# G = pp @ w for two f tiles in one step, the attention's small products next to it, the output product in thirds of K

## The chip, the core and the metric

One core of a Trainium2 chip. TensorE (PE) multiplies into PSUM; VectorE (DVE), ScalarE (ACT) and GpSimd (POOL) do the rest of the arithmetic, and SyncE (SP) issues the DMAs. The metric is the device time of one execution in microseconds (us). Before the change it is 772.41 us, the median of three runs (771.77 to 772.71).

## The reference

Eight batches of eight heads, sequence 576, head size 64. Per head, 32 packed queries `p` attend to `k`, `v`, and the queries `q` attend to what they gave; the result is the input of a gated feed-forward layer. All is float32.

```python
p_packed = sm_attn(p, k, v)            # (8, 8, 32, 64)
out = sm_attn(q, p_packed, p_packed)   # (8, 8, 576, 64)
x = out.transpose(0, 2, 1, 3).reshape(4608, 512)
return ((x @ w_a) * (x @ w_b)) @ w_out # w_a, w_b: 512 x 1536; w_out: 1536 x 512
```

## The kernel before

The second attention's weights, times `p_packed`, times `w_a`, are regrouped: G = pp @ w is built first (32 packed rows of each of eight heads, so 256 rows in two halves e of 128), and then x @ w_a and x @ w_b are a2 @ G, where a2 are the softmax weights of the second attention. The 1536 columns are cut into twelve f tiles of 128. Products of full precision are made of float32r parts, hi and lo: three matmuls for each product (hi hi, hi lo, lo hi).

Batches 0 and 1 run in an earlier stage of another form. The change concerns the loop over batches 2 to 7, which is written in *periods*, one for each f tile, 72 in all (`period`, L803). A period n holds

- `make_g` (L764): G of tile n + 2, eight small matmuls (L772) of 64 rows by 32 columns with 256 columns moving (128 for w_a, 128 for w_b), four heads r and two halves e, into the PSUM pair `s`;
- `sum_g` (L778): ACT, DVE and POOL form the sums `gs` that a product scheme with seven instead of eight block products needs; `split_g` (L788) cuts them into G_hi and G_lo, a third of a period later;
- seven block products (`product`, L754, matmuls at L759) of tiles n and n + 1 into the PSUM pairs `X` and `V`, each three matmuls with 288 columns;
- the steps that end a tile: d (ACT L821, DVE L824), c2 (ACT L832, DVE L847), the two halves of h = a * b, which are hf[1] on DVE (L837) and hf[0] on POOL (L848), and `split_h` (L793) of the tile before into h_hi (ACT L800) and h_lo (POOL);
- three *fills*: matmuls of the output product h @ w_out (`mm2_steps`, L718, matmuls at L722 with 512 columns), which run behind by half a batch. They accumulate six f tiles (half of K) of one 128-row tile in a bank of the PSUM pool `x` (two banks). The first half is copied by ACT to `part` (L728), the second is added to it by DVE (L732) and stored.

The next batch's attention is spread over the twelve periods by the strings in `STEPS` (L861), at three places in a period: behind the first, second and third fill. In them S is the first attention's score product (L255), r its following steps (the last of them the product with v, L299, all in the PSUM pair `s`), s the second attention's steps, the first of which is a product (L314), k and q transpositions on DVE, u the splitting of a2 into parts for the next batch (DVE a_lo and tx_lo, through `lo_part`, L92), t sums on POOL, L loads. The order on each engine is that in which this code is written (a manual schedule). G's weights are kept in DRAM (`w_kept`) by batch 1 and loaded for each f tile (`load_kept`, L698), 512 KB, into one of two buffers.

Of the kernel before, what the change touches and what calls it, by code (L numbers as in the profile page):

```python
# [8 lines left out]
F32 = mybir.dt.float32  # L9
# [10 lines left out]
def tile_packed_attn_gated_ffn(  # L20
# [568 lines left out]
    def keep_weights():  # L589

        c, u = divmod(kept[0], 2)
        nc.sync.dma_start(
            out=w_kept[kept[0]].rearrange("p (x f) -> p x f", f=P),
            in_=w_ab[:, c].rearrange("p r (a u f) -> p (r a) u f", a=2, u=2)[:, :, u, :])
        kept[0] += 1
# [38 lines left out]
    def tiles_of(b):  # L634
        return [64 + P * i for i in range(4)] if b % 2 == 0 else [P * i for i in range(5)]

    for b in range(NB):
# [33 lines left out]
        for i, c0 in enumerate(tiles):  # L671
# [7 lines left out]
            mm2_out(b, banks[i], c0, i)  # L679
    while kept[0] < NFT:  # L680
        keep_weights()
# [10 lines left out]
    part = lp.tile([P, NT, DO], F32, name="part")  # L692
    a_t = {(e, u): tuple(t[:, e, HS * u:HS * u + HS] for t in (a2_hi, a2_lo)) for e in range(E) for u in range(2)}
# [12 lines left out]
    load_kept(1)  # L706

# [9 lines left out]

    def mm2_steps(o, c0, fts, cols=slice(0, DO)):  # L718

        for ft in fts:  # L720
            for n, (ht, wt) in enumerate(((h_hi[ft], wo_hi[ft]), (h_hi[ft], wo_lo[ft]), (h_lo[ft], wo_hi[ft]))):
                nc.tensor.matmul(  # L722
                    out=o[:, cols], lhsT=ht[:, c0:c0 + P], rhs=wt[:, cols],
                    start=(ft == fts[0] and n == 0), stop=(ft == fts[-1] and n == 2))
                yield

    def keep_part(o, i):
        nc.scalar.copy(out=part[:, i], in_=o)  # L728

    def put_out(b, o, i, c0):  # L730
        ob = lp.tile([P, DO], F32, name="ob", bufs=2)
        nc.vector.tensor_tensor(out=ob, in0=o, in1=part[:, i], op=ALU.add)  # L732
        store(b, ob, c0)

    def mm2_half(b, half, tiles=None):

        for i, c0 in tiles or list(enumerate(tiles_of(b))):
            o = bank()
            yield from mm2_steps(o, c0, range(HF * half, HF * half + HF))
            if half == 0:  # L740
                pend.append(lambda o=o, i=i: keep_part(o, i))
            else:
                pend.append(lambda o=o, i=i, c0=c0: put_out(b, o, i, c0))

    filler = [iter(())]

    def fill(k):

        for _ in range(k):
            next(filler[0], None)  # L750
# [3 lines left out]
    def product(n, k, bank, first):  # L754

        j, (hi, lo) = PRODUCTS[k]
        gh, gl = G_hi[:, n % 3, j], G_lo[:, n % 3, j]
        for i, (g, t) in enumerate(((gh, hi), (gh, lo), (gl, hi))):
            nc.tensor.matmul(  # L759
                out=bank[:, n % 2, 0:HS], lhsT=g, rhs=t, start=(first and i == 0), stop=(i == 2), skip_group_check=True)  # L760
# [3 lines left out]
    def make_g(n):  # L764

        b = NB + n // NFT
        w = wr_of.pop(n)
        x = bank_pair(True)
        for r in range(R):
            for e in range(E):  # L770
                rows = slice(64 * e, 64 * e + 64)
                nc.tensor.matmul(  # L772
                    out=x[J * r:J * r + J, e, 0:2 * P], lhsT=ppT[rows, 2 * (b % 2), r, :], rhs=w[rows, r, :],
                    start=True, stop=True)
        load_kept(n + 2)
        return x

    def sum_g(n, x):  # L778

        nc.scalar.copy(out=gs[:, 0:2].rearrange("p a f -> p (a f)"), in_=x[:, 1, 0:2 * P])  # L780
        nc.scalar.copy(out=G_hi[:, n % 3, 0], in_=x[:, 0, 0:P])  # L781
        nc.vector.tensor_tensor(out=gs[:, 4], in0=x[:, 0, P:2 * P], in1=gs[:, 1], op=ALU.add)  # L782
        nc.vector.tensor_tensor(out=gs[:, 5], in0=gs[:, 4], in1=x[:, 0, 0:P], op=ALU.subtract)  # L783
        lo_part(G_lo[:, n % 3, 0], x[:, 0, 0:P], G_hi[:, n % 3, 0])
        nc.gpsimd.tensor_tensor(  # L785
            out=gs[:, 2:4], in0=gs[:, 0:2], in1=gs[:, 5:6].broadcast_to([P, 2, P]), op=ALU.subtract)

    def split_g(n):  # L788

        nc.scalar.copy(out=G_hi[:, n % 3, 1:7], in_=gs)  # L790
        lo_part(G_lo[:, n % 3, 1:7], gs, G_hi[:, n % 3, 1:7], nc.gpsimd)

# [10 lines left out]
    def period(n, fills, steps):  # L803
# [15 lines left out]
        if here or there:  # L819
            d = d_of[n] = lp.tile([P, 2, HS], F32, name="d", bufs=2)  # L820
            nc.scalar.copy(out=d[:, both], in_=X[:, both, 0:HS])  # L821
        fill(fills[0])
# [3 lines left out]
        emit_steps(b + 1, steps[0])  # L826
        if here:
# [17 lines left out]
        if here:  # L845
            c2 = c2_of.pop(n)
            nc.vector.tensor_tensor(out=c2, in0=V[:, k0, 0:HS], in1=c2, op=ALU.add)  # L847
            nc.gpsimd.tensor_tensor(out=hf[:, 0], in0=d_of.pop(n - 1)[:, k0], in1=c2, op=ALU.mult)  # L848
# [12 lines left out]
    STEPS = {0: ("S0 r0", "", "Lq1"), 1: ("S1 r1", "r0", ""), 2: ("r0", "r1", ""), 3: ("r0", "", "q0 Lv1"),  # L861
             4: ("r1", "", "q1 Lk2"), 5: ("r1", "P0", "Lv2 Lk3"), 6: ("s0 s0", "T2", "Lp4 s0"), 7: ("s1 s1", "s0", "s1"),
             8: ("s0", "s1", "s0"), 9: ("s1", "", "s1 t"), 10: ("", "u0", "u1 k2"), 11: ("", "u2", "u3 k3 Lq2")}
    banks_of["x"], banks_of["v"] = bank_pair(), bank_pair()
    for n in (-2, -1):
        period(n, (12, 12, 12) if n == -2 else (10, 8, 9), ("", "", ""))
    for n in range(LAST):
        b, ft = NB + n // NFT, n % NFT
        if ft % HF == 0:
            fill(99)  # L870
            flush()
            half_b = b if ft else b - 1
            filler[0] = mm2_half(half_b, 0 if ft else 1)
        period(n, (6, 4, 5) if half_b % 2 else (5, 3, 4), STEPS[ft])
    split_h(LAST - 1)
    fill(99)
    flush()
    last, tiles = B - 1, list(enumerate(tiles_of(B - 1)))
    filler[0] = mm2_half(last, 1, tiles[:-1])
    for _ in range(10):  # L880
        fill(9)
        flush()
    i, c0 = tiles[-1]
    ob = lp.tile([P, DO], F32, name="ob", bufs=2)
    for j in range(2):
        o = bank()
        cols = slice(j * DO // 2, (j + 1) * DO // 2)
        drain(mm2_steps(o, c0, range(HF, NFT), cols))
        nc.vector.tensor_tensor(out=ob[:, cols], in0=o[:, cols], in1=part[:, i, cols], op=ALU.add)
        store(last, ob, c0, cols)  # L890

# [29 lines left out]
```

## Time and profile before

| | |
|---|---|
| median of the runs | 772.41 us |
| the profiled execution | 773.32 us |
| its span, first to last instruction | 771.2 us |
| mean granted TensorE clock | 0.991 |
| PE busy with matmuls | 735.8 us |
| POOL / DVE / ACT busy | 471.8 / 420.6 / 362.8 us |
| moved by DMA | 102.47 MB, mean 133 GB/s |

Busy time is time in which an instruction of the engine is shown. Matmuls are pipelined: one starts before the one ahead is shown to end, so what a matmul costs is read from start to start. The loop of the periods runs from about 194 us to 740 us of the span; behind it stands the rest of the last batch's output product.

### The profile page before, as it was taken

Reading aid. Unit: us, or ns where it says so; the run is one execution under the profiler, and the core shown is the slowest. Engines: PE = TensorE matmul, PEld = TensorE weight load, DVE = VectorE, ACT = ScalarE, POOL = GpSimd, SP = SyncE. Lnnn points to the kernel's source line nnn. Section 1 sums busy time; section 2 is a strip of 40 time slices with the busy share of each in tenths; the row PEclk is TensorE's granted clock in tenths of the full one; section 3 lists DMA queues with packets and bytes.
Section 4 is the critical chain, followed back from the end, with each engine's and each line's share of the span. In section 5 each row is a group of like instructions: output and inputs, shape, how many; then the busy total and the mean of one; then the engine's idle time right before and its main releaser. Section 6 shows DMA issues by size and latency. Waiting matters only on the chain.

```text
span 771.2 us, 15740 instructions
## 1 busy us (share of the span) xinstructions
PE 735.8 (95%) x6140; PEld 573.5 (74%) x6140; DVE 420.6 (55%) x832; ACT 362.8 (47%) x760; POOL 471.8 (61%) x394
## 2 busy tenths in 40 slices
PE   6899999997999998999999998999999999899998
PEld 4488878975778766777777776677777777688887
DVE  2888564466245556555664556655664555544321
ACT  3778634533343454544544354453454335544430
POOL 0586652335165795667866688566875668777640
PEclk9999999998999999999999999999999999999999
DMA  8999937694335515373253732448144322123002
GB/s 247 376 239 290 247 68 155 161 245 127 86 108 147 162 60 116 110 183 109 83 119 111 184 120 74 104 136 189 68 107 107 118 107 83 55 96 124 28 1 69
DMA packets 193866, 102.47 MB, mean 133 GB/s; under 512 B 141953, under 2 KB 172417, under 8 KB 193793
## 3 DMA queue, kind: packets, MB, share of 16 engines
q1 hardware_dynamic: 193792, 101.47, 47.9%
q8 instruction: 49, 0.80, 0.4%
q14 instruction: 25, 0.20, 0.1%
HBM read 85.72 MB, written 15.73 MB: 132 GB/s over the span
## 4 chain that ended last, share of the span: by engine, by line
PE 71%; POOL 13%; DVE 7%; ACT 5%; issue 2%; DMA 1%; SPq 0%; DVEq 0%; POOLq 0%; ACTq 0%
PE x L722 25%; PE m L759 20%; PE m L384 9%; POOL G_lo L92 5%; PE m L410 4%; PE s L772 4%; POOL h_lo L92 2%; POOL t L332 2%; PE s L299 1%; POOL tf L602 1%; POOL asb L848 1%; PE s L314 1%; PE s L255 1%; DVE xT L125 1%; PE x L366 1%
## 5 line engine op out<-in xcount | busy, mean ns | idle before, releaser
L722 PE MATMUL x<-wo,h_hi 128*128 128x512 f32 (+1 forms) x780 | 249.4, 394 | 3.2 <-ACT part L728 3.2
L92 POOL TENSOR_TENSOR G_lo<-gs,G_hi 128x768 fp32r<-128x768 f32 x72 | 132.7, 1843 | 93.8 <-ACT G_hi L790 93.8
L92 POOL TENSOR_TENSOR h_lo<-asb,h_hi 128x576 fp32r<-128x576 f32 x96 | 138.7, 1445 | 50.7 <-ACT h_hi L403 46.9
L722 PEld LDWEIGHTS x<-wo,h_hi 128*128 128x128 f32 x780 | 141.5, 191 | 22.7 <-ACT part L728 3.7
L722 PE MATMUL x<-wo,h_lo 128*128 128x512 f32 (+1 forms) x390 | 153.0, 392 | 0.0
L759 PE MATMUL m<-a_hi,G_hi 128*128 128x288 f32 x288 | 98.6, 342 | 8.0 <-ACT d L821 4.5
L759 PEld LDWEIGHTS m<-a_hi,G_hi 128*128 128x128 f32 x288 | 54.2, 188 | 55.3 <-issue 35.8
L785 POOL TENSOR_TENSOR gs<-gs 128x256 f32<-128x256 f32 x72 | 53.0, 736 | 67.9 <-DVE gs L783 48.5
L780 ACT COPY gs<-s 128x256 f32<-128x256 f32 x72 | 26.8, 372 | 134.8 <-POOL G_lo L92 71.2
L759 PE MATMUL m<-a_lo,G_hi 128*128 128x288 f32 x288 | 85.8, 298 | 4.5 <-DVE a_lo L92 4.2
L759 PE MATMUL m<-a_hi,G_lo 128*128 128x288 f32 x288 | 86.0, 299 | 0.5 <-POOL G_lo L92 0.3
L722 PEld LDWEIGHTS x<-wo,h_lo 128*128 128x128 f32 x390 | 74.2, 190 | 12.0
L782 DVE TENSOR_TENSOR gs<-s,gs 128x128 f32<-128x128 f32 x72 | 20.6, 286 | 107.7 <-ACT G_hi L781 97.8
L824 DVE TENSOR_TENSOR d<-m,d 128x576 f32<-128x576 f32 (+1 forms) x73 | 54.7, 749 | 34.3 <-ACT d L821 22.0
L832 ACT COPY c<-m 128x288 f32<-128x288 f32 x72 | 28.7, 399 | 92.2 <-PE m L759 91.6
L848 POOL TENSOR_TENSOR asb<-d,c 128x288 f32<-128x288 f32 x72 | 61.0, 847 | 12.8 <-DVE c L847 12.8
L759 PE MATMUL m<-tx_hi,G_hi 128*128 128x288 f32 x216 | 64.8, 300 | 0.0
L790 ACT CAST G_hi<-gs 128x768 fp32r<-128x768 f32 x72 | 60.5, 841 | 7.7 <-POOL gs L785 7.7
L837 DVE TENSOR_TENSOR asb<-m,d 128x288 f32<-128x288 f32 x72 | 32.4, 450 | 57.9 <-ACT c L832 57.4
L759 PE MATMUL m<-tx_hi,G_lo 128*128 128x288 f32 x216 | 63.9, 296 | 0.0
L759 PE MATMUL m<-tx_lo,G_hi 128*128 128x288 f32 x216 | 63.8, 295 | 0.0
L800 ACT CAST h_hi<-asb 128x576 fp32r<-128x576 f32 x72 | 48.8, 678 | 26.5 <-POOL asb L848 26.3
(162 smaller groups left out, 1386.8 us busy)
## 6 DMA issues: line engine op xcount, KB each, us to landing
wr<-w_kept SPq DMA_DIRECT2D x72, 512.0 KB
nat<-in_k_dram SPq DMA_DIRECT2D x56, 144.0 KB
nat<-in_q_dram SPq DMA_DIRECT2D x56, 144.0 KB
vt<-in_v_dram SPq DMA_DIRECT2D x28, 256.0 KB
out_dram<-ob SPq DMA_DIRECT2D x27, 256.0 KB
raw<-in_moe_w_a_dram SPq DMA_DIRECT2D x12, 512.0 KB
raw<-in_moe_w_b_dram SPq DMA_DIRECT2D x12, 512.0 KB
raw<-in_moe_w_out_dram SPq DMA_DIRECT2D x12, 512.0 KB
```

The source lines that it names most:

```text
L92: return eng.tensor_tensor(out=dst, in0=src, in1=hi.bitcast(F32), op=ALU.subtract)
L384: nc.tensor.matmul(out=ps[:, half, 0:HS], lhsT=gt[:, kt, ft % 4, cols], rhs=at[:, kt, HS * half:HS * half + HS], start=(n == 0 and kt == 0 ...
L410: nc.tensor.matmul(out=o[:, cols], lhsT=ht[:, c0:c0 + P], rhs=wt[:, cols], start=(ft == 0 and n == 0), stop=(ft == NFT - 1 and n == 2))
L722: nc.tensor.matmul(out=o[:, cols], lhsT=ht[:, c0:c0 + P], rhs=wt[:, cols], start=(ft == fts[0] and n == 0), stop=(ft == fts[-1] and n == 2))
L759: nc.tensor.matmul(out=bank[:, n % 2, 0:HS], lhsT=g, rhs=t, start=(first and i == 0), stop=(i == 2), skip_group_check=True)
L772: nc.tensor.matmul(out=x[J * r:J * r + J, e, 0:2 * P], lhsT=ppT[rows, 2 * (b % 2), r, :], rhs=w[rows, r, :], start=True, stop=True)
L785: nc.gpsimd.tensor_tensor(out=gs[:, 2:4], in0=gs[:, 0:2], in1=gs[:, 5:6].broadcast_to([P, 2, P]), op=ALU.subtract)
L790: nc.scalar.copy(out=G_hi[:, n % 3, 1:7], in_=gs)
L800: nc.scalar.copy(out=view(h_hi[ft]), in_=src)
L824: nc.vector.tensor_tensor(out=d[:, both], in0=V[:, both, 0:HS], in1=d[:, both], op=ALU.add)
L837: nc.vector.tensor_tensor(out=hf[:, 1], in0=X[:, k0, 0:HS], in1=d[:, k0], op=ALU.mult)
L848: nc.gpsimd.tensor_tensor(out=hf[:, 0], in0=d_of.pop(n - 1)[:, k0], in1=c2, op=ALU.mult)
```

## The change

1. `make_g` runs in every second period, for two f tiles: eight matmuls with 512 columns instead of 256. One half e goes to one bank of the pool `x`, the other to the second, e = 1 first and r inside; `s` is left to the attention. `gs`, `A_hi`, `A_lo` (products 1 and 2, not split from `gs`) hold two tiles, G_hi and G_lo five blocks instead of seven.
2. `STEPS` has five places in a period; the first two stand ahead of and behind `make_g`. S0, the last steps of r0 and r1, S1 and the score products of s0 and s1 go there.
3. The output product is made in thirds of K (four f tiles). The first third is copied by ACT into one of five buffers `part`, the second is added in place by DVE, the third added and stored. Per pair of periods two or three tiles are filled, by `FILLS`.
4. hf[0] goes from POOL to DVE; `split_h` stands behind d instead of ahead of it; the attention's steps are spread anew.
5. Weights are kept and loaded for two f tiles at once, 1 MB, in one buffer.

```diff
-    w_kept = wdp.tile([NFT, P, R * 2 * P], F32, name="w_kept")
+    w_kept = wdp.tile([NC, P, R * 4 * P], F32, name="w_kept")
...
-            t = lp.tile([P, R, 2 * P], F32, name="wr", bufs=2)
-            nc.sync.dma_start(out=t.rearrange("p r f -> p (r f)"), in_=w_kept[n % NFT])
+            t = lp.tile([P, R, 4 * P], F32, name="wr")
+            nc.sync.dma_start(out=t.rearrange("p r f -> p (r f)"), in_=w_kept[n // 2 % NC])
...
+    def put_part(b, third, o, i, c0, cols=slice(0, DO)):
+        if third == 0:
+            nc.scalar.copy(out=parts[i], in_=o)
+            return
+        nc.vector.tensor_tensor(out=parts[i][:, cols], in0=o[:, cols], in1=parts[i][:, cols], op=ALU.add)
+        if third == 2:
+            store(b, parts[i], c0, cols)
...
-        x = bank_pair(True)
-        for r in range(R):
-            for e in range(E):
-                rows = slice(64 * e, 64 * e + 64)
+        gps = {}
+        for e in (1, 0):
+            gps[e] = bank()
+            rows = slice(64 * e, 64 * e + 64)
+            for r in range(R):
                 nc.tensor.matmul(
-                    out=x[J * r:J * r + J, e, 0:2 * P], lhsT=ppT[rows, 2 * (b % 2), r, :], rhs=w[rows, r, :],
+                    out=gps[e][J * r:J * r + J, :], lhsT=ppT[rows, 2 * (b % 2), r, :], rhs=w[rows, r, :],
                     start=True, stop=True)
...
+        nc.scalar.copy(out=gs[:, 0:2].rearrange("p a u f -> p (a u f)"), in_=x1)
+        a_parts = [[flat(t[:, e, n % 4:n % 4 + 2]) for t in (A_hi, A_lo)] for e in range(E)]
+        nc.scalar.copy(out=a_parts[0][0], in_=x0[:, 0:2 * P])
+        nc.scalar.copy(out=a_parts[1][0], in_=flat(gs[:, 0]))
+        s1, s2 = flat(gs[:, 4]), flat(gs[:, 5])
+        nc.vector.tensor_tensor(out=s1, in0=x0[:, 2 * P:4 * P], in1=flat(gs[:, 1]), op=ALU.add)
+        nc.vector.tensor_tensor(out=s2, in0=s1, in1=x0[:, 0:2 * P], op=ALU.subtract)
+        lo_part(a_parts[0][1], x0[:, 0:2 * P], a_parts[0][0])
+        lo_part(a_parts[1][1], flat(gs[:, 0]), a_parts[1][0], nc.gpsimd)
...
-        x = make_g(n + 2) if more else None
-        if more:
-            sum_g(n + 2, x)
-        split_h(n - 1)
+        emit_steps(b + 1, steps[0])
+        if more and n % 2 == 0:
+            make_g(n + 2)
+        emit_steps(b + 1, steps[1])
...
-            nc.gpsimd.tensor_tensor(out=hf[:, 0], in0=d_of.pop(n - 1)[:, k0], in1=c2, op=ALU.mult)
+            nc.vector.tensor_tensor(out=hf[:, 0], in0=d_of.pop(n - 1)[:, k0], in1=c2, op=ALU.mult)
...
+    FILLS = {2: ((5, 3, 4), (6, 6, 0)), 3: ((7, 5, 6), (9, 9, 0))}
```

Three places in the order of the instructions. First PE inside a batch. Before, S0's four rows (L255, into `s`) stand between the output product's matmuls (L722) and block products (L759), far from `make_g`:

```order
L722 MATMUL x<-wo,h_hi_506 128x512 x2
L722 MATMUL x<-wo,h_lo_507 128x512
L255 MATMUL s<-xT_2166,pT 32x288 x2
L255 MATMUL s<-xT_2203,pT 32x288 x2
L255 MATMUL s<-xT_2166,pT 32x288 x2
L255 MATMUL s<-xT_2203,pT 32x288 x2
L759 MATMUL m<-a_hi,G_hi 128x288
```

With the change, at the third period of a batch, r0's product with v (L298), `make_g` (L777) and S1 (L254) stand in a row between block products (L763):

```order
L763 MATMUL m<-tx_hi,G_lo 128x288
L298 MATMUL s<-vt,t_2478 32x64 x20
L777 MATMUL x<-wr,ppT 32x512 x8
L254 MATMUL s<-xT_2160,pT 32x288 x2
L254 MATMUL s<-xT_2202,pT 32x288 x2
L254 MATMUL s<-xT_2160,pT 32x288 x2
L254 MATMUL s<-xT_2202,pT 32x288 x2
L763 MATMUL m<-a_hi,G_hi 128x288
```

The small products have moved against each other, and no block or output product stands between them.

Second, PE at the start of the loop's code, where the first `make_g` stands. Before, it follows 18 matmuls of one output tile (six f tiles, h_hi_492 to h_lo_503) and writes `s`:

```order
L722 MATMUL x<-wo,h_lo_501 128x512
L722 MATMUL x<-wo,h_hi_502 128x512 x2
L722 MATMUL x<-wo,h_lo_503 128x512
L772 MATMUL s<-wr,ppT 32x256 x8
L722 MATMUL x<-wo,h_hi_492 128x512 x2
L722 MATMUL x<-wo,h_lo_493 128x512
```

With the change it follows 24 matmuls of two output tiles (four f tiles each) and writes both banks `x`:

```order
L720 MATMUL x<-wo,h_lo_499 128x512
L777 MATMUL x<-wr,ppT 32x512 x8
L720 MATMUL x<-wo,h_hi_492 128x512 x2
L720 MATMUL x<-wo,h_lo_493 128x512
L720 MATMUL x<-wo,h_hi_494 128x512 x2
```

The matmuls behind it now need a bank that `make_g` has written, and those ahead of it have held the same two.

Third, DVE in one period. Before, c2 (L847) is followed by the G sums (L782, L783) and d (L824):

```order
L847 TENSOR_TENSOR c_2425<-m,c_2425 128x288
L782 TENSOR_TENSOR gs<-s,gs 128x128
L783 TENSOR_TENSOR gs<-gs,s 128x128
L92 TENSOR_TENSOR G_lo<-s,G_hi 128x128
L824 TENSOR_TENSOR d<-m,d 128x576
L837 TENSOR_TENSOR asb<-m,d 128x288
L732 TENSOR_TENSOR ob<-x,part 128x512
```

With the change hf[0] (L857) stands behind c2 (L856), the sums (L788, L789) are twice as wide, and the add of a third (L730) stands ahead of c2:

```order
L730 TENSOR_TENSOR part_2177<-x,part_2177 128x512
L856 TENSOR_TENSOR c_2603<-m,c_2603 128x288
L857 TENSOR_TENSOR asb<-d,c_2603 128x288
L304 TENSOR_SCALAR pp<-s,rs 128x64
L788 TENSOR_TENSOR gs<-x,gs 128x256
L789 TENSOR_TENSOR gs<-gs,x 128x256
L91 TENSOR_TENSOR A_lo<-x,A_hi 128x256
L833 TENSOR_TENSOR d<-m,d 128x576
```

DVE's queue has one more multiplication in each period, ahead of everything of the next one.

More of the change, by code (lines that the diff above doesn't have):

```diff
@@ L589, in keep_weights @@
     def keep_weights():
[L591 to L594, printed above, removed]
+        nc.sync.dma_start(out=w_kept[kept[0]], in_=w_ab[:, kept[0]].rearrange("p r f -> p (r f)"))
         kept[0] += 1
@@ L679, in tile_packed_attn_gated_ffn @@
             mm2_out(b, banks[i], c0, i)
-    while kept[0] < NFT:
+    while kept[0] < NC:
         keep_weights()
@@ L716, in flush, with mm2_steps, mm2_third, tiles_at @@
             pend.pop(0)()
-    def mm2_steps(o, c0, fts, cols=slice(0, DO)):
+    def mm2_steps(o, c0, fts, then, cols=slice(0, DO)):
         for ft in fts:
             for n, (ht, wt) in enumerate(((h_hi[ft], wo_hi[ft]), (h_hi[ft], wo_lo[ft]), (h_lo[ft], wo_hi[ft]))):
+                end = ft == fts[-1] and n == 2
                 nc.tensor.matmul(
-                    out=o[:, cols], lhsT=ht[:, c0:c0 + P], rhs=wt[:, cols],
-                    start=(ft == fts[0] and n == 0), stop=(ft == fts[-1] and n == 2))
+                    out=o[:, cols], lhsT=ht[:, c0:c0 + P], rhs=wt[:, cols], start=(ft == fts[0] and n == 0), stop=end)
+                if end:
+                    pend.append(then)
                 yield
[L727 to L737, printed above, removed]
-            o = bank()
[L739 to L743, printed above, removed]
+    def put_part(b, third, o, i, c0, cols=slice(0, DO)):
[5 more added lines that the diff above has]
+            store(b, parts[i], c0, cols)
+    def mm2_third(b, third, tiles):
+        for i, c0 in tiles:
+            o = bank()
+            yield from mm2_steps(
+                o, c0, range(4 * third, 4 * third + 4), lambda o=o, i=i, c0=c0: put_part(b, third, o, i, c0))
+    def tiles_at(b, ft):
+        b, third, half = {0: (b - 1, 1, 1), 2: (b - 1, 2, 0), 4: (b - 1, 2, 1),
+                          6: (b, 0, 0), 8: (b, 0, 1), 10: (b, 1, 0)}[ft]
+        tiles = list(enumerate(tiles_of(b)))
+        n = (len(tiles) + 1) // 2
+        return b, third, tiles[n:] if half else tiles[:n]
     filler = [iter(())]
@@ L774, in make_g @@
                     start=True, stop=True)
         load_kept(n + 2)
[L776 to L784, printed above, removed]
+        flat = lambda t: t.rearrange("p x f -> p (x f)")
@@ L791, in split_g @@
-        lo_part(G_lo[:, n % 3, 1:7], gs, G_hi[:, n % 3, 1:7], nc.gpsimd)
+        nc.scalar.copy(out=G_hi[:, n % 3], in_=gs[:, 1:6, n % 2])
+        lo_part(G_lo[:, n % 3], gs[:, 1:6, n % 2], G_hi[:, n % 3], nc.gpsimd)
     def split_h(n):
@@ L878, in tile_packed_attn_gated_ffn, with rest @@
     last, tiles = B - 1, list(enumerate(tiles_of(B - 1)))
-    filler[0] = mm2_half(last, 1, tiles[:-1])
-    for _ in range(10):
-        fill(9)
+    def rest():
+        yield from mm2_third(last, 1, tiles[3:])
+        yield from mm2_third(last, 2, tiles[:-1])
+    filler[0] = rest()
+    for _ in range(9):
+        fill(12)
         flush()
     i, c0 = tiles[-1]
-    ob = lp.tile([P, DO], F32, name="ob", bufs=2)
     for j in range(2):
```

59 lines of the change are left out of this document (33 added, 26 removed), and 3 rows, old and new, of the table STEPS.

## The prediction

> **What bounds the kernel now.** I read the page first, for shares; then the list of waits of PE; then the timeline of PE alone, for the price of each step.
>
> ```profile
> PE 735.8 (95%) x6140; PEld 573.5 (74%) x6140; DVE 420.6 (55%) x832; ACT 362.8 (47%) x760; POOL 471.8 (61%) x394
> ...
> PE 71%; POOL 13%; DVE 7%; ACT 5%; issue 2%; DMA 1%; SPq 0%; DVEq 0%; POOLq 0%; ACTq 0%
> ```
>
> PE is the bound: 95% busy, and 71% of the chain that ended last. Another 25% of the chain lies on POOL, DVE and ACT, at places where PE waits for them. The waits of PE, in us of idle time, times, and the longest:
>
> ```profile
> PE s L255 <- DVE G_lo L92: 5.0, 5, 1.3
> PE m L759 <- ACT d L821: 4.5, 10, 0.7
> PE m L759 <- DVE a_lo L92: 4.2, 3, 1.4
> ...
> PE m L759 <- DVE c L847: 3.5, 5, 1.4
> PE x L722 <- ACT part L728: 3.2, 1, 3.2
> ...
> PE s L772 <- DMA wr<-w_kept: 0.8, 1, 0.8
> ```
>
> These are small against 771 us. So the time can fall in two ways: PE does the same work in fewer or cheaper steps, or these waits go.
>
> **One small burst for G, before.** `make_g` of one f tile (L772) is 8 instructions, 16 rows of the trace, between two wide streams (start us, duration, engine, line, tiles, shapes, count):
>
> ```profile
> 429.22 0.62 PE L722 MATMUL x<-wo,h_hi 128*128 128x512 f32 x2
> 429.68 0.39 PE L722 MATMUL x<-wo,h_lo 128*128 128x512 f32 x1
> 429.99 0.66 PE L772 MATMUL s<-wr,ppT 64*32 64x256 f32 x16
> 430.58 0.40 PE L759 MATMUL m<-a_hi,G_hi 128*128 128x288 f32 x1
> 430.82 0.29 PE L759 MATMUL m<-a_lo,G_hi 128*128 128x288 f32 x1
> 430.95 0.29 PE L759 MATMUL m<-a_hi,G_lo 128*128 128x288 f32 x1
> ```
>
> Starts matter, not durations. Undisturbed, a 512-wide matmul starts every 0.23 us (two in 429.22 to 429.68) and a 288-wide one every 0.13 (430.82 to 430.95). From 429.68 to 430.82 PE does one wide matmul, the burst and one product: 1.14 - 0.23 - 0.13 = **0.78 us** for the burst, of which about 0.09 is the late entry (0.31 to 0.32 in place of 0.23) and 0.11 the slow first product behind it (0.24 in place of 0.13).
>
> **The same for two f tiles.** The loop of before has no 512-wide burst, but its first stage has:
>
> ```profile
> 54.95 0.69 PE L384 MATMUL m<-a_hi,glo 128*128 128x288 f32 x4
> 55.57 1.09 PE L366 MATMUL x<-w_ab,ppT 64*32 64x512 f32 x16
> 56.59 0.53 PE L384 MATMUL m<-a_hi,ghi 128*128 128x288 f32 x2
> 56.96 0.43 PE L384 MATMUL m<-a_lo,ghi 128*128 128x288 f32 x2
> ```
>
> The fourth L384 starts at 54.95 + 0.40 = 55.35; from there to 56.96 are three products (0.40) and the burst: 1.61 - 0.40 = **1.21 us**. Two tiles cost 2 x 0.78 = 1.56 before and 1.21 after: 0.35 us a pair. The loop has 72 f tiles, 36 pairs: **-12.6 us**.
>
> **The attention's bursts beside it.** The change puts S0, r0's and r1's last product, S1, s0 and s1 of the next batch against a `make_g`: six a batch, and five batches of the loop have a next one, so 30. Alone, S0 (L255) costs 208.73 - 207.53 = 1.20, less 0.23 and 0.13: 0.84 us.
>
> ```profile
> 207.53 0.39 PE L722 MATMUL x<-wo,h_lo 128*128 128x512 f32 x1
> 207.85 0.72 PE L255 MATMUL s<-xT,pT 64*32 64x288 f32 x16
> 208.49 0.40 PE L759 MATMUL m<-a_hi,G_hi 128*128 128x288 f32 x1
> 208.73 0.29 PE L759 MATMUL m<-a_lo,G_hi 128*128 128x288 f32 x1
> ```
>
> Three such bursts stand together in the stage ahead of the loop:
>
> ```profile
> 129.39 0.72 PE L255 MATMUL s<-xT,pT 64*32 64x288 f32 x16
> 130.04 0.67 PE L366 MATMUL m<-w_ab,ppT 64*32 64x256 f32 x16
> 130.50 1.07 PE L366 MATMUL x<-w_ab,ppT 64*32 64x512 f32 x16
> 131.50 0.54 PE L384 MATMUL m<-a_hi,ghi 128*128 128x288 f32 x2
> 131.87 0.43 PE L384 MATMUL m<-a_lo,ghi 128*128 128x288 f32 x2
> ```
>
> 129.39 to 131.87, less two products and plus the entry, is 2.30; apart they would be 0.84 + 0.78 + 1.21 = 2.83. Two joints save 0.53, 0.27 each. From below a joint saves its late entry and slow product, 0.19; from above the 0.35 of a pair. I take the row: 30 x 0.27 = **-8.1 us** (5.7 to 10.5).
>
> The new burst goes through the four heads r of one half e before the other half; before, the halves alternated. S0 has the new order (half u outside, r inside), and its 16 rows still give way to the next product after 0.64 us (207.85 to 208.49), so I cost the order at nothing. [...]
>
> **Work of the vector engines.** None of it is on PE's path by itself. In the groups of instructions below the last columns are busy us, mean ns of one, and idle time before them. Thirds in place of halves add one DVE add for each of 32 output tiles, 0.69 us by the row of L732: 22 us, spread over 560 us on an engine that is 55% busy. ACT's narrow copies for G become half as many of twice the width: nothing. hf[0] leaves POOL, where six instructions a pair replace eight:
>
> ```profile
> L92 POOL TENSOR_TENSOR h_lo<-asb,h_hi 128x576 fp32r<-128x576 f32 x96 | 138.7, 1445 | 50.7 <-ACT h_hi L403 46.9 <-ACT h_hi L800 2.4 <-DMA nat<-in_q_dram 1.1
> L92 POOL TENSOR_TENSOR G_lo<-gs,G_hi 128x768 fp32r<-128x768 f32 x72 | 132.7, 1843 | 93.8 <-ACT G_hi L790 93.8
> ...
> L848 POOL TENSOR_TENSOR asb<-d,c 128x288 f32<-128x288 f32 x72 | 61.0, 847 | 12.8 <-DVE c L847 12.8
> ...
> L785 POOL TENSOR_TENSOR gs<-gs 128x256 f32<-128x256 f32 x72 | 53.0, 736 | 67.9 <-DVE gs L783 48.5 <-ACT h_hi L800 7.1 <-ACT d L821 5.7
> ...
> L732 DVE TENSOR_TENSOR ob<-x,part 128x512 f32<-128x512 f32 x31 | 21.2, 685 | 18.5 <-PE x L722 18.4
> ```
>
> Before: 2 x (1.45 + 0.74 + 0.85 + 1.84) = 9.8 us a pair. After, by the slope between 256, 576 and 768 columns (about 2.1 ns a column): h_lo 2 x 1.45, gs 1.3, A_lo 0.74, G_lo with 640 columns 2 x 1.58: 8.1 us. POOL gains 1.7 us a pair.
>
> hf[0] on DVE has two operands in SBUF. The nearest operation on DVE is a_lo, of the same 288 columns:
>
> ```profile
> L92 DVE TENSOR_TENSOR a_lo<-t,a_hi x26: 441/738/2084, 114.3 to 670.8; 128x288 fp32r<-128x288 f32 x24, 128x576 fp32r<-128x576 f32 x2
> ```
>
> It takes 0.44 us at best and 2.08 at worst. I take 0.44 to 2.08 for hf[0] and put nothing on PE for it: behind it on DVE stand the gs sums and the next d, and PE needs that d only for the last products of the next period, at least nine products and nine wide matmuls (3.3 us) later. If that cover went, the excess of 1.64 us would fall on PE. [...]
>
> **The waits.** A wait costs PE its idle time plus about 0.16, since a matmul shown with 0.39 us is followed after 0.23.
> - S0 waits for the bank `s` that `make_g` filled. Now `make_g` uses `x` and `s` is free: 5.0 idle, and 5 x 0.07, as the idle time begins after 0.39 and the natural entry is 0.32: **-5.4**.
> - d (10), a_lo (3), c (5): 12.2 + 18 x 0.16 = 15.1 us. d is late where ACT's gs copy waits for POOL to have read gs:
>
> ```profile
> ACT gs L780 <- POOL G_lo L92: 71.2, 39, 2.8
> ```
>
> That copy now comes once a pair, POOL has less to do, and h's split stands behind d: I let d's 6.1 go. The a_lo steps stand a third of a period earlier, but a transposition and the wide gs work share DVE with them, and c follows them there: half of 9.0. **-10.6** (0 to -15.1).
> - The start of the loop gets worse. PE stands from 183.24 to 186.86 while ACT works off casts that come from POOL, the gs copy and a copy of the second product's bank:
>
> ```profile
> 173.51 0.63 PE L722 MATMUL x<-wo,h_hi 128*128 128x512 f32 x2
> ...
> 183.24 0.39 PE L722 MATMUL x<-wo,h_lo 128*128 128x512 f32 x1
> ...
> 185.79 0.36 ACT L780 COPY gs<-s 128x256 f32<-128x256 f32 x1
> ...
> 186.86 1.22 PE L722 MATMUL x<-wo,h_hi 128*128 128x512 f32 x2 [3.24 <-ACT part L728]
> ```
>
> Now the first burst itself lies in the two `x` banks, and the next wide matmul needs the gs copy out of one. PE gets there after 24 wide matmuls and the burst, 173.51 + 24 x 0.23 + 1.2 = 180.2. ACT's queue ahead of that copy is the same, so the copy, now 0.6 us wide, ends near 186.4: PE stands 6.2 us, where before it lost 3.4 and 0.9 (the kept weights' DMA). **+1.9** (-4.0 to +4).
> - TensorE's granted clock is halved three times: after that wait, and twice for 3.4 us behind a long wait for a_lo (one is shown; the 0.50 is the clock).
>
> ```profile
> 185.80:192.60 6.80, 5.74 (x14) 4.48 (x15) 1.76 (x6) 2.32 (x6) 2.56 (x2) 0.50 0.16 63
> 291.60:295.00 3.40, 3.40 (x12) 2.66 (x11) 2.66 (x5) 1.21 (x2) 2.13 (x3) 0.50 0.39 62
> ```
>
> At half clock 3.4 us hold 1.7 us of work. I let one of the two later ones go: **-1.7** (0 to -3.4).
>
> Weights come as 1 MB for a pair into one buffer instead of 0.5 MB twice into two; the load has a pair's time, some 13 us, and PE waited for such a load once, 0.8 us. Nothing. If that cover went, PE would wait at the burst each pair.
>
> **Sum.** The profiled execution took 773.3 us (span 771.2 and 2.1 around it), 0.9 above the median 772.41. 773.3 - 12.6 - 8.1 - 5.4 - 10.6 - 1.7 + 1.9 = 736.8, so **737**.
>
> **Rivals.**
> 1. *Only the bursts pay.* The old waits come back in other places: DVE's longer queue, both banks of `x` held by G. 773.3 - 20.7 + 2 = 755; with part of the waits gone 742 to 755. For it: waits so short that moving work on four engines makes new ones. Chance 0.26.
> 2. *All waits of the loop go:* 773.3 - 20.7 - 5.4 - 15.1 - 3.4 + 2 = 731, and 722 at the least (joints at 0.35, which is -2.4, and the start's two waits, 4.0, gone in place of +2). For it: POOL's relief. Chance 0.18.
> 3. *Slower by the shared banks.* `make_g` can begin only when both `x` banks are read. DVE's add frees one, and behind the last wide matmul PE has only six products (0.8 us) to cover it. If DVE is held up by POOL once a pair, 2.08 - 0.44 = 1.64 us, then 36 x 1.64 = 59: 796. It decides from 36 / 36 = 1.0 us a pair on. Against it: the add stands ahead of hf[0] in DVE's queue. Chance 0.03.
> 4. [...] Chance 0.02.
>
> **Numbers.** Forecast (732 to 742) 0.50, rivals 0.26, 0.18, 0.03, 0.02, and 0.01 for no change. The ends are 722 (rival 2) and 757 (773.3 - 12.6 - 5.7 + 2, with every wait replaced), which hold some 0.9 by my cases; I cut nothing, since the unknown waits have no nearer bound. 0.2% is about what a measurement can tell from no change: faster by more 0.95, within 0.01, slower 0.04.
>
> **What would show it.** PE's 512-wide bursts in the loop, 36 of them at about 1.2 us; S0 directly ahead of one and no idle time before it; POOL busy some 60 us less; hf[0] on DVE between 0.44 and 2.1 us. I am wrong if PE waits for a bank, for gs or for c in every pair, if the joints save under 0.19, or if the half-clock stretches grow in number.

## The result, and the profile after

The changed kernel takes **738.88 us** (median of 4 runs, 738.49 to 739.75); the kernel before, run beside it, 772.56 (771.77 to 773.34). The ratio is **0.9566**, 95% interval 0.9549 to 0.9582. The profiled execution took 738.6 us, its span is 736.8, and the mean granted clock of TensorE is 0.995 (0.991 before).

The busy times and the chain that ended last, on the page of the changed kernel:

```profile
PE 707.6 (96%) x5558; PEld 574.3 (78%) x5558; DVE 474.8 (64%) x828; ACT 359.9 (49%) x724; POOL 424.6 (58%) x322
...
PE 75%; POOL 9%; DVE 5%; ACT 3%; DMA 3%; issue 3%; SPq 1%; DVEq 0%; POOLq 0%; ACTq 0%
```

PE has 582 matmul rows fewer (576 of them `make_g`'s, 36 x 16 instead of 72 x 16) and is 28 us less busy; POOL gave up 47 us and DVE took 54. On the chain, POOL fell from 13% to 9%. What PE still waits for (us of idle time, times, the longest):

```profile
PE m L763 <- ACT d L829: 6.0, 10, 0.9
PE x L720 <- ACT gs L783: 5.6, 1, 5.6
...
PE m L763 <- DVE tx_lo L91: 1.0, 2, 0.5
PE m L763 <- POOL G_lo L91: 0.8, 1, 0.8
...
PE s L254 <- DVE xT L124: 0.5, 1, 0.5
PE x L777 <- DMA wr<-w_kept: 0.5, 1, 0.5
PE m L763 <- DVE c L856: 0.3, 2, 0.2
```

S0's wait for the bank is gone: the entry for xT lies at 60 us, ahead of the loop. Those for a_lo and c have shrunk from 7.7 us to 1.3 (tx_lo and c). The wait for the weights `wr` lies at 438 us, inside the loop. And d stands there ten times, as before, and for longer. On the timeline of PE, one `make_g` alone and one behind a step of the attention (start, duration, engine, line, tiles, shapes, count):

```profile
278.04 0.30 PE L763 MATMUL m<-tx_hi,G_lo 128*128 128x288 f32 x1
278.26 1.09 PE L777 MATMUL x<-wr,ppT 64*32 64x512 f32 x16
279.28 0.40 PE L763 MATMUL m<-a_hi,G_hi 128*128 128x288 f32 x1
279.52 0.29 PE L763 MATMUL m<-a_lo,G_hi 128*128 128x288 f32 x1
```

```profile
264.02 0.30 PE L763 MATMUL m<-tx_hi,G_lo 128*128 128x288 f32 x1
264.25 0.72 PE L313 MATMUL s<-xT,ppT 64*32 64x288 f32 x16
264.76 1.06 PE L777 MATMUL x<-wr,ppT 64*32 64x512 f32 x16
265.75 0.40 PE L763 MATMUL m<-a_hi,G_hi 128*128 128x288 f32 x1
265.99 0.30 PE L763 MATMUL m<-a_lo,G_hi 128*128 128x288 f32 x1
```

Counted as in the prediction, from the start of the product ahead to that of the second product behind, less two products of 0.13: alone 279.52 - 278.04 - 0.26 = 1.22 us; with s1's scores ahead 265.99 - 264.02 - 0.26 = 1.71.

### The profile page after: what moved, and what is told of

The parts are those of the page before. It is cut to its first block, busy times and chain, and to the rows that moved or that the text cites. A ratio compares the mean times of both kernels' runs of the same rounds, so it can differ in the third digit from the quotient of the medians.

```text
span 736.8 us, 14156 instructions
## 1 busy us (share of the span) xinstructions
PE 707.6 (96%) x5558; PEld 574.3 (78%) x5558; DVE 474.8 (64%) x828; ACT 359.9 (49%) x724; POOL 424.6 (58%) x322
## 4 chain that ended last, share of the span: by engine, by line
PE 75%; POOL 9%; DVE 5%; ACT 3%; DMA 3%; issue 3%; SPq 1%; DVEq 0%; POOLq 0%; ACTq 0%
PE x L720 30%; PE m L763 21%; PE m L383 8%; PE m L409 5%; PE x L777 4%; POOL G_lo L91 3%; DMA wr<-w_kept 2%; POOL h_lo L91 2%; POOL t L323 1%; PE s L298 1%; PE s L254 1%; PE s L313 1%; POOL t L331 1%; PE x L365 1%; ACT gs L783 1%
## 5 line engine op out<-in xcount | busy, mean ns | idle before, releaser
L91 POOL TENSOR_TENSOR h_lo<-asb,h_hi 128x576 fp32r<-128x576 f32 x96 | 141.7, 1476 | 114.7 <-ACT h_hi L808 58.9
L91 POOL TENSOR_TENSOR G_lo<-gs,G_hi 128x640 fp32r<-128x640 f32 x72 | 114.2, 1586 | 47.5 <-ACT G_hi L798 47.5
L91 POOL TENSOR_TENSOR A_lo<-gs,A_hi 128x256 fp32r<-128x256 f32 x36 | 27.8, 773 | 77.3 <-ACT A_hi L786 77.3
L829 ACT COPY d<-m 128x576 f32<-128x576 f32 (+1 forms) x73 | 46.5, 637 | 52.0 <-PE m L763 35.2
L730 DVE TENSOR_TENSOR part<-x,part 128x512 f32<-128x512 f32 (+1 forms) x65 | 44.1, 679 | 36.3 <-PE x L720 36.2
L763 PE MATMUL m<-tx_hi,G_lo 128*128 128x288 f32 x216 | 63.8, 296 | 0.8 <-POOL G_lo L91 0.8
L763 PE MATMUL m<-tx_hi,G_hi 128*128 128x288 f32 x216 | 64.5, 299 | 0.0
L763 PE MATMUL m<-tx_lo,G_hi 128*128 128x288 f32 x216 | 63.5, 294 | 1.0 <-DVE tx_lo L91 1.0
L783 ACT COPY gs<-x 128x512 f32<-128x512 f32 x36 | 21.1, 587 | 87.7 <-PE x L777 73.0
L763 PEld LDWEIGHTS m<-a_hi,G_hi 128*128 128x128 f32 x144 | 27.0, 187 | 43.7 <-issue 18.2
L857 DVE TENSOR_TENSOR asb<-d,c 128x288 f32<-128x288 f32 x72 | 58.0, 805 | 2.5
L798 ACT CAST G_hi<-gs 128x640 fp32r<-128x640 f32 x72 | 52.8, 733 | 13.0 <-POOL gs L792 13.0
L763 PE MATMUL m<-a_hi,G_hi 128*128 128x288 f32 x144 | 48.7, 338 | 6.1 <-ACT d L829 6.0
L792 POOL TENSOR_TENSOR gs<-gs 128x512 f32<-128x512 f32 x36 | 46.7, 1296 | 0.1
```

The costliest lines, as they stand in the source:

```text
L91: return eng.tensor_tensor(out=dst, in0=src, in1=hi.bitcast(F32), op=ALU.subtract)
L730: nc.vector.tensor_tensor(out=parts[i][:, cols], in0=o[:, cols], in1=parts[i][:, cols], op=ALU.add)
L763: nc.tensor.matmul(out=bank[:, n % 2, 0:HS], lhsT=g, rhs=t, start=(first and i == 0), stop=(i == 2), skip_group_check=True)
L792: nc.gpsimd.tensor_tensor(out=gs[:, 2:4].rearrange("p a u f -> p a (u f)"), in0=gs[:, 0:2].rearrange("p a u f -> p a (u f)"), in1=s2.unsqu ...
L798: nc.scalar.copy(out=G_hi[:, n % 3], in_=gs[:, 1:6, n % 2])
L857: nc.vector.tensor_tensor(out=hf[:, 0], in0=d_of.pop(n - 1)[:, k0], in1=c2, op=ALU.mult)
```

## Experiments

All but one are edits of the changed kernel. Each was run beside the kernel before; ratios are to that. The kernel before took 771.76 to 772.66 us in these groups, so a difference between the medians of two groups is good to about 1 us.

**1. The attention's bursts back in the middle of the period** (`joints_undone`)

```diff
-    STEPS = {0: ("S0", "", "r0", "r0 Lq1", "Lv1"), 1: ("", "", "r0", "", ""), 2: ("r0", "S1", "r1", "r1", ""),
-             3: ("", "", "q0 r1", "", "Lk2"), 4: ("r1", "", "", "P0", ""), ...
-             6: ("s0", "", "s0", "s0", "s0"), 7: ("", "", "s0", "s0", ""), 8: ("s1", "", "s1", "s1", "s1"),
+    STEPS = {0: ("", "", "S0 r0", "r0 Lq1", "Lv1"), 1: ("", "", "r0", "", ""), 2: ("", "", "r0", "S1 r1", "r1"),
+             3: ("", "", "q0 r1", "", "Lk2"), 4: ("", "", "r1", "P0", ""), ...
+             6: ("", "", "s0 s0", "s0", "s0"), 7: ("", "", "s0", "s0", ""), 8: ("", "", "s1 s1", "s1", "s1"),
```

> The changed kernel with the attention's six bursts of a batch back in the middle of the period, away from make_g. Theory (a joint of two bursts saves PE one late entry and one slow first product): six joints in each of five batches come apart again; the profile of the changed kernel shows 1.88 us a batch for them, so +9.4 us, 748 us; the prediction's row of 0.27 a joint would give +8.1, 747. The exponentials keep their place nearly, so the ten waits for d stay. Rival (what a joint saves is lost elsewhere or was never there): 739, within 1.5 us of the changed kernel.

746.14 us, ratio 0.9668 (0.9650 to 0.9685): 7.3 us slower than the changed kernel, span 744.4. A score burst (s0) by itself on its timeline:

```profile
255.59 0.61 PE L720 MATMUL x<-wo,h_hi 128*128 128x512 f32 x2
256.13 0.72 PE L313 MATMUL s<-xT,ppT 64*32 64x288 f32 x16
256.78 0.40 PE L763 MATMUL m<-a_hi,G_hi 128*128 128x288 f32 x1
257.01 0.29 PE L763 MATMUL m<-a_lo,G_hi 128*128 128x288 f32 x1
```

The second wide matmul starts at 255.59 + 0.23 = 255.82; to 257.01, less 0.23 and 0.13, are 0.83 us. Apart, the two bursts cost 0.83 + 1.22 = 2.05; together 1.71: a joint saves **0.34 us**, and 30 of them 10.2. Another kind agrees: r1's product with v costs 1.02 by itself in `joints_undone`, and 1.88 together with `make_g` in the changed kernel, where apart they would be 1.02 + 1.22 = 2.24. Only 7.6 of span came back, because the waits for d became shorter at the same time:

```profile
PE m L763 <- ACT d L829: 3.4, 10, 0.4
```

6.0 - 3.4 = 2.6, and 7.6 + 2.6 = 10.2 (smaller differences nearly cancel: 0.7 us less of waits for xT, `wr` and the inputs, 1.1 more at the start of the loop). The theory holds; its sum lacked the waits. They are ten in both kernels, so the joints did not make them, though with the joints they are longer.

**2. The exponential behind d** (`exp_late`)

```diff
-             6: ("s0", "", "s0", "s0", "s0"), 7: ("", "", "s0", "s0", ""), 8: ("s1", "", "s1", "s1", "s1"),
-             9: ("", "", "s1 k2", "s1", "t"), ...
+             6: ("s0", "", "s0", "s0", ""), 7: ("", "", "s0", "s0", "s0"), 8: ("s1", "", "s1", "s1", ""),
+             9: ("", "", "s1 k2", "s1", "s1 t"), ...
```

> The changed kernel with the exponential of the softmax (ACT, L325) emitted one step later, behind the copy of d in the next period. Theory: eight of the ten waits of PE for d come from ACT's queue, where the exponential stands ahead of d and waits for POOL's subtraction. They go: 8 x (0.6 + 0.16) = -6.1 us, 732.7 us, and the list of waits of PE shows d twice instead of ten times. Rival (d is late because ACT has too much to do, or because of the bank): the waits stay or move to another product, 738.9 us within 1.5.

First the place in the changed kernel, on the timeline of POOL, ACT, DVE and PE:

```profile
256.86 1.59 POOL L91 TENSOR_TENSOR G_lo<-gs,G_hi 128x640 fp32r<-128x640 f32 x1
...
257.49 1.27 DVE L857 TENSOR_TENSOR asb<-d,c 128x288 f32<-128x288 f32 x1
...
258.39 1.39 POOL L323 TENSOR_TENSOR t<-t,mx 128x576 f32<-128x576 f32 x1
...
259.82 0.69 ACT L325 ACTIVATE t<-t 128x576 f32<-128x576 f32 x1 [1.30 <-POOL t L323]
260.41 0.62 ACT L829 COPY d<-m 128x576 f32<-128x576 f32 x1
...
261.08 0.40 PE L763 MATMUL m<-a_hi,G_hi 128*128 128x288 f32 x1 [0.61 <-ACT d L829]
```

Read it upwards: PE waits for the copy of d, the copy stands in ACT's queue behind the exponential (L325), and this waits 1.30 us for POOL's subtraction (L323), which stands behind G_lo.

In the edit the exponential and the two steps behind it each move one place later. Measured: 735.20 us, ratio 0.9527 (0.9507 to 0.9546), 3.7 us faster than the changed kernel and not 6.1. On the timelines the loop gains 4.9 us, and its start loses 0.8. PE's waits:

```profile
PE m L763 <- ACT d L829: 2.3, 3, 1.5
PE m L763 <- DVE tx_lo L91: 1.9, 3, 0.8
PE m L763 <- POOL G_lo L91: 1.7, 2, 0.8
...
PE m L763 <- DVE c L856: 1.1, 2, 0.6
```

The eight waits are gone, so their cause is shown. The two of the changed kernel that had another cause remain; there d's copy waits for hf[0], as the changed kernel's timeline has it:

```profile
288.10 0.64 ACT L829 COPY d<-m 128x576 f32<-128x576 f32 x1 [0.46 <-DVE asb L857]
...
288.79 0.41 PE L763 MATMUL m<-a_hi,G_hi 128*128 128x288 f32 x1 [0.24 <-ACT d L829]
```

One more wait for d, of 1.46 us, came in elsewhere (at 628.34 us; there the cast of G_hi ahead of d waits 4.27 us for POOL's gs), and PE waits 2.6 us longer for G_lo, tx_lo and c than in the changed kernel: part of the gain was given back behind the next late engine.

**3. One wide burst as two narrow ones** (`two_narrow`)

```diff
-            for r in range(R):
-                nc.tensor.matmul(out=gps[e][J * r:J * r + J, :], ..., rhs=w[rows, r, :], ...)
+        for c in (0, 2 * P):
+            for e in (1, 0):
+                for r in range(R):
+                    nc.tensor.matmul(out=gps[e][J * r:J * r + J, c:c + 2 * P], ..., rhs=w[rows, r, c:c + 2 * P], ...)
```

> The changed kernel with make_g in two halves of 256 columns one behind the other, into the same banks: 16 instructions, 32 rows, instead of 8 of 512 columns. Theory (the pair gains one late entry and one slow first product, not the width): the time of the changed kernel, 739 us, 0 to +3 us. Rival (the gain is in the wide instruction itself): two single bursts again, up to 36 x 0.35 = +12.6, 751 us. In between, the two share the gain.

739.66 us, ratio 0.9586 (0.9568 to 0.9605): 0.8 us above the changed kernel, and the intervals overlap. Its timeline:

```profile
278.94 0.29 PE L763 MATMUL m<-tx_hi,G_lo 128*128 128x288 f32 x1
279.16 1.09 PE L779 MATMUL x<-wr,ppT 64*32 64x256 f32 x32
...
280.42 0.30 PE L763 MATMUL m<-a_lo,G_hi 128*128 128x288 f32 x1
```

32 rows of 256 columns take the same 1.48 us from 278.94 to 280.42 as 16 rows of 512. The width of an instruction gains nothing: **the pair's gain is a joint**, one way in and one way out instead of two, the same 0.34 us as in experiment 1.

**4. The first `make_g` in the banks of `s`** (`start_in_s`)

```diff
+        pair = bank_pair(True) if n == 0 else None
...
-            gps[e] = bank()
+            gps[e] = bank() if pair is None else pair[:, e, :]
```

> The changed kernel with the first make_g of the loop alone in the two banks of s instead of the two of x. Theory (PE stands 5.6 us at the start of the loop because the next wide matmul needs a bank of x that the gs copy must first read): the wait of 5.6 us goes, and the first window at half clock behind it may go too (3.4 us): 730 to 735 us. Rival (PE then stands nearly as long for the next thing that ACT has not worked off, the part copy or G_hi): 737 to 739 us, with a wait of some 3.2 us for the part copy as before the change.

731.99 us, ratio 0.9485 (0.9467 to 0.9504), 6.9 us faster than the changed kernel. The wait is now one for the `part` copy, and shorter than either kernel's:

```profile
PE x L720 <- ACT part L728: 1.7, 1, 1.7
```

With 5.6 us of standing PE also had the half clock behind it. In the rows by windows (the numbers with (x) are busy time of PE, PEld, DVE, ACT and POOL, then the granted clock) the changed kernel has

```profile
179.00:185.00 6.00, 2.05 (x18) 0.31 (x16) 5.65 (x7) 1.95 (x5) 4.40 (x6) 0.84 0.60 94
185.00:192.00 7.00, 5.39 (x17) 4.38 (x18) 3.04 (x7) 2.96 (x9) 2.32 (x3) 0.65 0.42 153
```

and `start_in_s`, behind its 1.7 us,

```profile
187.50:191.00 3.50, 3.44 (x17) 2.92 (x18) 0.58 (x2) 1.58 (x4) 2.66 (x3) 1.00 0.26 108
```

In the changed kernel half clock lasts to 189.9, and PE runs again from 186.6: 3.3 us at half clock, which cost 1.6. So 3.9 us of idle time and 1.6 of clock went. On the timelines the start gains 5.8 us, and the wait for `wr` inside the loop, 0.7 with its restart, is gone too: 6.5, the difference of the spans.

**5. hf[0] back on POOL** (`hf0_pool`, and once more as `hf0_pool_again`)

```diff
-            nc.vector.tensor_tensor(out=hf[:, 0], in0=d_of.pop(n - 1)[:, k0], in1=c2, op=ALU.mult)
+            nc.gpsimd.tensor_tensor(out=hf[:, 0], in0=d_of.pop(n - 1)[:, k0], in1=c2, op=ALU.mult)
```

> The changed kernel with hf[0] back on POOL, as before the change. POOL gets 72 x 0.85 = 61 us of work more, DVE 58 less. Theory (POOL's relief is worth something because the softmax subtraction on POOL is what the exponential, and behind it d, wait for): the eight waits for d behind the exponential grow by up to 0.85 each, and the rest of POOL's chain (G_lo, h_lo) comes later too: +3 to +8 us, 742 to 747. Rival (POOL has slack everywhere; the move did nothing): 739 within 1.5. Third (hf[0] on DVE did harm, because ACT's copy of d waits 16.8 us in 11 places for it, d having two buffers): these waits go and the time falls by 1 to 3 us.

753.58 us, ratio 0.9749 (0.9735 to 0.9763): **14.7 us slower** than the changed kernel, nearly twice the theory's upper end. A second run of the same kernel gives the profile:

> The kernel of hf0_pool once more, for a profile at full clock: its own was taken at a granted clock of 0.56 throughout. It was 14.7 us slower than the changed kernel, where the theory had 3 to 8. Theory now (every wait that follows POOL's chain grows, not only the eight behind the exponential): the list of waits of PE shows d more often than 10 times or longer, and new entries for G_lo, tx_lo, c or xT, together some 14 us more than in the changed kernel. Rival (the time is lost in the clock: longer waits open half-clock windows): the mean granted clock is below 0.99 and half of the 14.7 us lies there.

751.39 us (750.12 and 752.65), ratio 0.9722 (0.9640 to 0.9805). PE's waits, and under them ACT's:

```profile
PE m L763 <- ACT d L829: 17.2, 13, 3.4
```

```profile
ACT d L829 <- POOL asb L857: 47.3, 19, 3.0
```

In the changed kernel the second row reads:

```profile
ACT d L829 <- DVE asb L857: 16.8, 11, 2.1
```

d has two buffers. hf[0] of period n reads the d of period n - 1, and ACT's copy in period n + 1 writes the same buffer: it must wait for hf[0]. On POOL, behind gs and G_lo, hf[0] comes so late that the copy and PE with it stand still. The third theory was the wrong way round: on DVE hf[0] does hold ACT up, but on POOL it does so nearly three times as long. PE's waits for d grew by 11.2 us. The clock took some 4.7 (mean 0.989, in the changed kernel 0.995): two new stretches at half clock stand in the loop behind long waits for d (3.3 us of work lost; one is shown in the last section), and the one at the start is longer (1.4). Against that, the waits for tx_lo, G_lo, xT and `wr` are gone (2.8 us). So both explanations of the expectation are true in part, the waits for the larger one; but of the waits that the theory named only those for d and c grew.

**6. hf[0] alone to DVE, in the kernel before** (`before_hf0_dve`): the same line at L848, the other way.

> The kernel before the change with hf[0] alone on DVE. Theory of the prediction (POOL's relief takes away the waits of the loop for d, and for a_lo and c): the waits for d (6.1 us with their restarts) go, and up to half of the 9.0 of a_lo and c: -6 to -10 us, ratio 0.987 to 0.992. Rival (the waits for a_lo and c went because make_g's wide work comes once a pair and at another place, the wait for d is ACT's queue): 0 within 2 us, ratio 0.998 to 1.002, and the waits stay in the list.

766.20 us, ratio 0.9913 (0.9892 to 0.9933): 6.5 us faster than the kernel before. Its list of waits has no entry for ACT's d any more, while the others stay:

```profile
PE s L255 <- DVE G_lo L92: 4.6, 4, 1.5
PE m L759 <- DVE c L847: 4.2, 5, 1.6
...
PE m L759 <- DVE a_lo L92: 3.4, 3, 1.2
```

The d waits of before (4.5 idle and ten restarts, 6.1) are nearly the whole gain. So none of the ten comes about without hf[0] on POOL, and it has no part in those for c, a_lo and the bank. What was queued ahead of d in the kernel before, on ACT's timeline:

```profile
382.56 0.37 ACT L780 COPY gs<-s 128x256 f32<-128x256 f32 x1 [0.85 <-POOL G_lo L92]
...
384.58 0.67 ACT L800 CAST h_hi<-asb 128x576 fp32r<-128x576 f32 x1 [1.48 <-POOL asb L848]
385.16 0.63 ACT L821 COPY d<-m 128x576 f32<-128x576 f32 x1
```

It is the cast of h, which waits for hf[0]. Four of the ten places look like this, with 1.1 to 1.8 us of waiting in the cast. In the other six, at 276.78 us for one, it is the gs copy that waits for POOL's G_lo, 2.4 to 2.8 us, as the prediction has it, and the cast behind it waits only 0.2 more for hf[0]. The gs copy's waits alone do not make PE wait: without hf[0] on POOL they are as long in sum (73.1 us, 71.2 before), and PE's waits for d are gone.

**7. The two halves of the rows in turn** (`halves_in_turn`)

```diff
-        for e in (1, 0):
-            for r in range(R):
+        for r in range(R):
+            for e in (1, 0):
```

> The changed kernel with make_g's eight products in the order of before, the two halves e of the rows in turn instead of four of one half and then four of the other. By the trace (a burst of 16 rows of 512 columns takes 1.0 us in the new order, as in the first stage, which has the other order): no difference, 739 within 1.5 us. [...]

738.96 us, ratio 0.9562 (0.9550 to 0.9574): no difference to the changed kernel. The burst has the same rows:

```profile
278.13 0.29 PE L763 MATMUL m<-tx_hi,G_lo 128*128 128x288 f32 x1
278.35 1.09 PE L778 MATMUL x<-wr,ppT 64*32 64x512 f32 x16
...
279.61 0.29 PE L763 MATMUL m<-a_lo,G_hi 128*128 128x288 f32 x1
```

1.48 us again: the four heads of one half in a row cost no more than the halves in turn. Why, no run here tells.

**8. Both repairs** (`both_fixes`): experiments 2 and 4 together.

> The changed kernel with the exponential one step later and the first make_g in the banks of s, both. If the two causes are separate, the gains measured alone add: 738.9 - 3.7 - 6.9 = 728.3 us. If they share a cause, 731 to 733.

**728.71 us** (727.62 to 730.54), ratio **0.9431** (0.9415 to 0.9446): the gains add, and this is faster than both kernels.

## Why the prediction was right, step by step

It said 737 and the kernel takes 738.9. Its terms, from rows of before and after (us; a wait is idle time and 0.16 for each time):

| term | predicted | measured |
|---|---|---|
| 36 pairs | -12.6 | 36 x (1.56 - 1.22) = -12.2 |
| 30 joints | -8.1 | 30 x 0.34 = -10.2 |
| S0's wait for the bank | -5.4 | -5.4 (none left in the loop) |
| waits for d, a_lo and c (with G_lo) | -10.6 | -5.0 |
| start of the loop | +1.9 | 5.7 - 4.3 = +1.4 |
| load of the weights, 1 MB for a pair | 0 | +0.6 (one wait for `wr`) |
| half clock | -1.7 | -3.4, and -1.2 at the start = -4.6 |
| sum | -36.5 | -35.4 |

The profiled executions differ by 773.3 - 738.6 = 34.7, so the terms hold 0.7 us too much. Ahead of the loop 0.6 us less of waiting for DMAs and a new wait for xT of 0.7 cancel.

That the sum came within 2 us is in part luck. The term for the waits of the loop was wrong by 5.6 us, and the joints (2.1 us more than predicted) and the clock (2.9 more) made up for most of it.

*The bursts.* Size and mechanism were right: late entry and slow first product, once instead of twice. The joint was put at 0.27 from one row of three bursts; it is 0.34, the upper bound that the prediction gave (0.35). Experiments 1 and 3 show that pair and joint are one thing.

*S0's wait* went as predicted, mechanism and size: the bank of `s` is free. It stayed in experiment 6, whose `make_g` still fills `s`.

*The waits of the loop* are the step that failed. The prediction let all of d's 6.1 go and half of the 9.0 for a_lo and c. It came out the other way: a_lo and c are down to 1.3 idle and four restarts, 1.9, and d rose to 7.6. One more, for G_lo, went from 0.5 to 1.0. "d is late where ACT's gs copy waits for POOL to have read gs" was only the front of the chain: in all ten places the last thing ahead of d was h's cast, waiting for hf[0] on POOL (experiment 6). Those waits did go, by parts of the change that the prediction named: hf[0] on DVE is enough by itself (experiment 6); h's split behind d was not tried alone. Then eight new ones came in the place where the new table puts the softmax exponential into ACT's queue ahead of d (experiment 2), and two more where d's copy waits for hf[0] on DVE. The prediction looked at what leaves ACT's queue ahead of d, not at what enters it. This is its first rival in small, for one wait out of four.

*hf[0]* was put at nothing. On PE's path its duration is nothing indeed: 0.46 to 1.54 us, between the bounds. But its place is worth 6.5 us in the kernel before and 14.7 in the one after, because of whom it frees: ACT's copy of d. POOL's relief was 47 us, where the prediction had some 60: the rows show 7.6 of the difference in POOL's own instructions that take longer, h_lo 141.7 us in all instead of 138.7, the softmax subtraction 18.8 instead of 16.6, the tf sums 17.1 instead of 14.7.

*a_lo and c.* The runs show what does not make them: neither the joints (experiment 1: 1.0 and 0.4 remain) nor hf[0] on POOL (experiment 6: they stay). The rows of the kernel before point to what does, though no edit tried it. Each of the three a_lo that PE waits for starts on DVE while POOL's G_lo runs, and takes 1.77 us instead of 0.44 (the row holds two a_lo; the first ends at 290.15, 0.32 behind G_lo):

```profile
288.01 1.82 POOL L92 TENSOR_TENSOR G_lo<-gs,G_hi 128x768 fp32r<-128x768 f32 x1
...
288.38 2.14 DVE L92 TENSOR_TENSOR a_lo<-t,a_hi 128x288 fp32r<-128x288 f32 x2 [2.54 <-ACT a_hi L616]
...
290.20 0.40 PE L759 MATMUL m<-a_lo,G_hi 128*128 128x288 f32 x1 [1.41 <-DVE a_lo L92]
```

All five waits for c stand right behind such an a_lo (1.77 or 2.08 us) in DVE's queue. In the changed kernel no a_lo of the loop takes more than 1.13 us. There it is tx_lo that falls beside G_lo, and the two waits for tx_lo stand behind ones of 1.51. The prediction took the spread of the a_lo row, 0.44 to 2.08, for hf[0], and did not see it behind the waits for a_lo. The u steps have other places in the change; moving them alone was not tried.

*The start* was right: PE stands 5.6 us (6.2 predicted) because both `x` banks hold G, and experiment 4 shows the bank to be the cause. *The clock:* both later windows at half speed went with the long waits for a_lo, where the prediction let one go. At the start PE ran 5.7 us at half clock behind its wait, and now 3.3, which is 1.2 us that the prediction didn't count. This term belongs to the profiled execution (mean clock 0.991): others of the kernel before have mean clocks up to 0.996.

The other rivals: the waits of the loop did not all go (the second; its 731 us is passed only with both repairs), no wait for a bank in every pair (the third), no difference by the order of the halves (the fourth; experiment 7 has 738.96 us in the order of before). The cost of thirds on DVE, and of the 1 MB loads, was put at nothing. No row but the one wait for `wr` contradicts it; they were not tried by themselves.

## What to carry to other kernels

A burst of small matmuls between wide ones had a price at its two ends here, 0.34 us for a way in and a way out, and it was saved by laying bursts side by side, not by making their instructions wider (`two_narrow`: 1.48 us either way). When a wait is to go, list everything that stands in the queue of the late engine ahead of what is waited for, before and after the change: the new order brings its own, here eight waits for d behind the exponential. And a small operation on a busy engine may be dear through the buffer that it keeps from being overwritten: hf[0], 0.85 us on POOL, was worth 6.5 and 14.7 us by its place.

## What the runs showed of the hardware

- hf[0] on DVE, which has two operands in SBUF, takes longer under an instruction of POOL. In the changed kernel it takes 0.46 us at best, 0.60 in the median and 1.54 at worst. The 39 of 72 that take more than 0.5 us all start while a POOL instruction runs; the other 33, all at 0.46, start with POOL idle or less than 0.1 us from the end of its instruction. In the rows of experiment 2 hf[0] starts at 257.49, under POOL's G_lo, which ends at 258.45, and takes 1.27 us to 258.76. For POOL the rows show less: the softmax subtraction (128x576, 14 times) takes 1.18 us on average in the kernel before and in `hf0_pool_again`, with hf[0] on POOL, and 1.34 in the changed kernel and in `before_hf0_dve`, with hf[0] on DVE. Why, the runs do not tell.
- The length of a wait alone does not tell whether half clock follows it. In `hf0_pool_again` PE waits 2.63 us for d, to 292.73, and the granted clock is 1.00 from there to 300. In the kernel before half clock follows a wait of only 1.41 us for a_lo. The clock records of the kernel before and of the changed one change only at times that lie whole multiples of 3.41 us apart; in the kernel before these are 185.76, 192.58, 291.57, 294.98, 663.62 and 667.04 us. Cut into windows of 3.41 us by these times, the span shows the following. The wait of 1.41 us, with one of 0.30 for c behind it, left PE busy for half of its window, 1.70 us, and half clock followed at 291.57 (the row at 291.60 in the prediction). The row ahead of it, nearly that window, is

```profile
288.00:291.50 3.50, 1.79 (x9) 1.25 (x10) 3.12 (x5) 1.79 (x6) 2.37 (x3) 1.00 0.43 150
```

  The wait of 2.63 us is divided between two windows of its run, in which PE is busy for 2.05 and 2.10 us. A wait of 3.42 us in the same run fills one, and half clock follows:

```profile
643.00:646.50 3.50, 0.11 (x1) 0.00 (x0) 2.07 (x1) 0.66 (x2) 2.81 (x3) 0.99 0.00 0
646.50:650.00 3.50, 3.47 (x11) 3.10 (x12) 2.65 (x3) 2.24 (x5) 1.95 (x2) 0.52 0.00 0
```

  Two cases lie close to each other by the busy time: in `start_in_s`, around its wait of 1.7 us, 3.50 us with PE busy for 1.87 (184.00 to 187.50) have full clock behind them (the row in experiment 4), and the 3.50 us with 1.79 above have half clock. No experiment varied this by itself.
